# Feed-forward gradients turned by DMA instead of TensorE, and attention's output turned one stage earlier

## The chip, the cores and the metric

The kernel runs on one core of a Trainium2 chip. The metric is the device time of one execution in microseconds (us): before the change the median of three runs is 2908.62 us (2898.36 to 2910.74). PE is TensorE (PEld its weight loads), DVE is VectorE, ACT is ScalarE, POOL is GpSimd and SP is SyncE. SP and POOL also issue the transfers, each in its own order; a transfer that waits holds up all that stands behind it on the same queue. "Turned" means transposed: from token-major (a token per partition) to feature-major, or back.

## What is computed

The reference is one transformer layer and its gradient: 2048 tokens of width 448.

```python
def _fwd_reference(...):
    h = x + _A_ref(_layernorm(x), mem0, Wq, Wk, Wv, Wo)     # attention in 64 segments of 32 tokens; the first
                                                            # 8 output rows of a segment are the next one's memory
    g = silu(layernorm(h) @ w_gate)                         # 448 -> 1792
    u = layernorm(h) @ w_up
    return h + (g * u) @ w_down                             # 1792 -> 448

def reference(..., grad_out):
    out, vjp = jax.vjp(forward, x, mem0, Wq, Wk, Wv, Wo, w_gate, w_up, w_down)
    return out, *vjp(grad_out)
```

In the feed-forward block's backward pass the gradient dz = grad_out @ w_down.T gives the gradients of the gate's input (dgp) and of u (du); the gradient of the normed h is dgp @ w_gate.T + du @ w_up.T.

## The kernel before, in words

Everything is written out by hand in program order (`tc.manual_schedule()`), so the order in which the code issues work is the order of each engine's queue. There are four stages: the forward chain of attention, the feed-forward tiles (forward and backward in one), the backward chain of attention, and a tail of weight gradients.

*Forward chain* (`forward_chain`). 64 steps, one a segment, each depending on the step before through the memory rows; four steps make a token tile of 128. A step projects q, k and v (L561, L569), moves v's rows into the layout that attention reads (`v_shift`: some rows by copies on POOL, L527, some by small transfers on SP, L758; `v_b_rows`, L754, for the memory rows), computes scores and probabilities, multiplies with v (L932) and applies Wo (L690). At the end of nearly every step `w_turn` (L772) has SP turn two 128-column pieces of a weight matrix from DRAM by a transposing DMA; at the start of the next step `w_store` (L766) has POOL store the result, and waits for it. In a tile's first step POOL also loads the input rows `T.x2` (L814), in two buffers in turn; they are read in the third step of the next tile (`out_ev`). After a tile's fourth step POOL stores the tile's attention output feature-major (OTA, 1024 KB, L981).

*Feed-forward tiles* (`ffn_phase`). 16 tiles of 128 tokens, taken in the order ORD. The loop runs over i = 0 to 13; in pass i the tile t has its backward part, the next tile n1 its forward part, and tile n2 is loaded. On PE a pass is: `dz(t)` (16 matmuls, L1128), `down_mm(t)` (14, L1180, reads the turned z in `ff.zT`), `dh_out(t-1)` (L1225), `gate(n1)` and `up(n1)` (32, L1128), `dh_turn(t)` (28 transposes by PE of dgp and du, L1166, evicted by ACT to `ff.dgpT` and `ff.duT`, L1079), `dout_turn(n1)` and `hn_turn(n2)` (L1108), and `dh_mm(t)` (28 matmuls, L1208, 14 over dgpT and 14 over duT). DVE makes dgp (L1193) and du (L1196) in `grads(t)` after dz, and z (L1151) in `up(n1)`; it reads dh_mm's result in `dh_ln` (from L216 on). On SP a pass has the three loads of tile n2 (L1092 to L1095), then for i = 1 to 12 the transposing DMA of z into `ff.zT` (L1303), then for i = 3 to 13 `o_turn(3)`: up to three transposing DMAs (L1243), each of half a tile of OTA, 128 x 1024, from DRAM into one of three buffers, and on POOL a store of each into OTok, the token-major copy that the tail reads (L1244). POOL's other stores of a pass are DH and DHb (L1215, L1218), DGP and DU (L1194, L1197), HN, Zt and the output. In pass i = 2 `load_back` has SP turn Wo from DRAM for the backward chain (four transposing DMAs, L1053 and L1054), with a memset on POOL that waits for them (L1055). In pass i = 10 the backward chain's first loads are issued.

The two matmul sums of `down_mm` and `dh_mm` stand in two fixed PSUM banks (`k.fix`); `dgp`, `du`, `ff.dgpT`, `ff.duT` and `ff.zT` are one buffer each.

Of the kernel before, what the change touches and what calls it, by code (L numbers as in the profile page):

```python
# [10 lines left out]
BF16 = mybir.dt.bfloat16  # L11
# [4 lines left out]
P = 128  # L16
# [81 lines left out]
@43264 oA#1:8192 oB#1:2048  # L98
@54016 V_sb:4096 hA:2048
@61184 part:2048 partB:2048 Vev:2048 aT#1:1024  # L100
xtmp:1024x2 x2load:1024x2 P_sb1:1024 S_sb:640x2 maskr:640 maskf:160 hB#1:256
@76032 wturn:1792"""
FFN = """WdT:14336
h_ld:896x3 hn:1024x3 dout_ld#2:1024x2 dh_t:1792 lnb_prod:1792 lnb_t1:1792 dh_b:896 o_t:896x2
# [392 lines left out]
def forward_chain(k: _K, hA, NWIN, Wq_sb, Wk_sb, Wv_sb, Wo_sb, maskr, work, stage, ff, feed, srcs):  # L497
    nc, tc = k.nc, k.tc
# [132 lines left out]
    def b_units(t, which):  # L631
        W_sb = {"k": Wk_sb, "q": Wq_sb, "v": Wv_sb}[which]
        T = tiles[t]
        st = {}

        def stat(kc):
            return T.hB[0:DB, kc, :, :]

        def mm(ps, half, kcs=range(4)):
            if which == "v":  # L640
                proj_v(ps, stat, half, kcs)
            else:
                proj(ps, W_sb, stat, half, kcs)

        def u1():
            st["p0"] = ps1(FP32)
            mm(st["p0"], 0)

        def e1():
            tg = "bevv" if which == "v" else "bev"  # L650
            st["ev"] = stage.tile([P, GF], BF16, name=tg, tag=tg, bufs=2)
            A(st["ev"][:, 0:HB], st["p0"][:, :])

        def u2():
            st["p1"] = ps1(FP32)
            mm(st["p1"], 1, range(0, 2))

        def u3():
            mm(st["p1"], 1, range(2, 4))

        def e3():
            V(st["ev"][:, HB:GF], st["p1"][:, :])
            if which == "v":
                T.vB = st["ev"]
            else:
                nc.gpsimd.dma_start(out=dr["KtokB" if which == "k" else "QtokB"][t], in_=st["ev"][:])

        def ut():
            if which == "v":
                return  # L670
            pt = ps1(BF16)
            for j in range(NJ):
                nc.tensor.transpose(pt[:, j * P:(j + 1) * P], st["ev"][:, j * P:(j + 1) * P], ident[:, :])  # L673
            st["pt"] = [pt[:, half * HB:(half + 1) * HB].rearrange("p (j g t) -> p j g t", j=4, g=G) for half in range(2)]

        def et():
            if which == "v":
                return
            dst = stage.tile([P, MC, SEG], BF16, name=which + "B", tag=which + "B", bufs=2)
            for half in range(2):  # L680
                A(fm_view(dst, half, 0, SEG), st["pt"][half])
            setattr(T, which + "B", dst)
        return dict(u1=u1, e1=e1, u2=u2, u3=u3, e3=e3, ut=ut, et=et)
# [43 lines left out]
    def none_units():  # L727
        def f():
            pass
        return dict(u1=f, e1=f, u2=f, u3=f, e3=f, ut=f, et=f)  # L730
# [33 lines left out]
    def w_store():  # L764
        for w, c, b in held:
            nc.gpsimd.dma_start(out=dr["WT"][w][:, c:c + 2, :], in_=b)  # L766
        held.clear()

    def w_turn():
        w, c = ahead.pop(0)  # L770
        b = work.tile([P, 2, D], BF16, name="wturn", bufs=1)
        nc.sync.dma_start_transpose(out=b, in_=wsrc[w][:, c * P:(c + 2) * P])  # L772
        held.append((w, c, b))
# [29 lines left out]
    for s in range(NSEG):  # L803
# [3 lines left out]
        if r == 0:  # L807
            if t + 1 < NT:
                tiles[t + 1] = tok_tile(t + 1)
            T.aT = stage.tile([P, KC, P], BF16, name="aT_tile", tag="aT", bufs=2)  # L810
            T.oA = stage.tile([P, MC, P], BF16, name="oA", tag="oA", bufs=2)
            T.oB = stage.tile([P, MC, SEG], BF16, name="oB", tag="oB", bufs=2)
            T.x2 = work.tile([P, DP], BF16, name="x_t2", tag="x2load", bufs=2)
            nc.gpsimd.dma_start(out=T.x2[:, 0:D], in_=X2[t * P:(t + 1) * P, :])  # L814
            cur = o_units(t - 1) if t > 0 else none_units()
        else:
            cur = b_units(t + 1, "?kqv"[r]) if t + 1 < NT else none_units()

        def stat(kc):
            return hA[0:DB, kc, sl, :]  # L820
# [93 lines left out]
            (nc.gpsimd if final else nc.sync).dma_start(out=dr["Vtok"][s, gg], in_=V_sb[QB * gg:QB * gg + 48, :])  # L914
        if s != NSEG - 3 and ahead:
            w_turn()
        if s == NSEG - 3:
            next(feed)

# [63 lines left out]
        late2 = late  # L983
        late = cur

    assert not ahead and not held
    uo["e3"]()
    next(feed)
    uo["ut"]()
# [70 lines left out]
def ffn_phase(k: _K, WT, ff, work, mv2, rstd2, srcs, back):  # L1060
# [127 lines left out]
    def grads(t):  # L1188
        o = T[t]
        dg = work.tile([P, F], BF16, name="scr", bufs=1)  # L1190
        nc.vector.tensor_tensor(out=dg[:], in0=o.dz[:], in1=o.u[:], op=ALU.mult)
        o.dgp = work.tile([P, F], BF16, name="dgp", bufs=1)
        nc.vector.tensor_tensor(out=o.dgp[:], in0=dg[:], in1=o.sg[:], op=ALU.mult)  # L1193
        nc.gpsimd.dma_start(out=dr["DGP"][rows(t), :], in_=o.dgp[:])  # L1194
        o.du = work.tile([P, F], BF16, name="du", bufs=1)
        nc.vector.tensor_tensor(out=o.du[:], in0=o.dz[:], in1=o.g[:], op=ALU.mult)  # L1196
        nc.gpsimd.dma_start(out=dr["DU"][rows(t), :], in_=o.du[:])  # L1197

    def dh_turn(t):
        turn_f(T[t].dgp, ff.dgpT, (A, A))  # L1200
        turn_f(T[t].du, ff.duT, (A, A))
# [31 lines left out]
        A(dT[:], pt[:, 0:KC * P])  # L1233
        nc.gpsimd.dma_start(out=dr["doutT"][t], in_=dT[:])

    quarters = [(t, q) for t in range(NT) for q in range(2)]

    def o_turn(n):
        for t, q in quarters[:n]:
            b = ff.ot[len(quarters) % 3]  # L1240
            del quarters[0]
            cols = slice(q * 1024, (q + 1) * 1024)
            nc.sync.dma_start_transpose(out=b.rearrange("n (c p) -> n c p", p=P), in_=dr["OTA"][t][:, cols])  # L1243
            nc.gpsimd.dma_start(out=dr["OTok"][t][:, cols], in_=b)  # L1244
# [34 lines left out]
    for i in range(NT - 2):  # L1279
        t, n1, n2 = ORD[i:i + 3]  # L1280
        if i > 0:
            load(n2)
        if i == 2:
            load_back(k, WT["o"], srcs["o"], True)
        if i == NT - 6:
            next(back)
        if not 1 < i < NT - 2:
            turn_f(T[t].z, ff.zT, (A, A))
        dz(t)
        if i > 0:  # L1290
            dh_ln(t - 1)
        down_mm(t)
        if i == 0:
            rstd(NT - 1, NT)
        grads(t)
        if i > 0:
            dh_out(t - 1)
        gate(n1)
        down_ev(t)
        norm(n2)  # L1300
        up(n1)
        if 0 < i < NT - 3:
            nc.sync.dma_start_transpose(out=ff.zT, in_=T[n1].z)  # L1303
        if 2 < i < NT - 2:
            o_turn(3)
        if i == NT - 3:
            dout_turn(n1)
            hn_turn(n2)
            gate(n2)
            load_back(k, WT["v"], dr["WT"]["v"], False, 0, HC)  # L1310
            up(n2)
            load_back(k, WT["v"], dr["WT"]["v"], False, HC, 2 * HC)
            dh_turn(t)
            slope(n1)
            slope(n2)
        else:
            dh_turn(t)
            dout_turn(n1)
            hn_turn(n2)
            slope(n1)  # L1320
        dh_mm(t)
# [783 lines left out]
```

## Time and profile before

| | |
|---|---|
| Median of three runs | 2908.62 us (2898.36 to 2910.74) |
| The profiled execution | 2923.15 us, of it a span of 2921.0 us |
| Mean granted TensorE clock | 0.986 |
| PE / DVE / ACT / POOL busy | 93% / 53% / 37% / 28% of the span |
| Forward chain | about 73 to 963 us |
| Feed-forward tiles | about 963 to 1295 us |
| Backward chain, then tail | from about 1312 us, the tail from about 2236 us |

In the profile's rows "L1208" is line 1208 of the kernel before. A row of the timeline gives start, length, engine, line, operation, "written <- read" by the program's names, the count, and in brackets how long the engine sat idle before and what ended it. Names such as `arena` and `wall` are large areas in which tiles are placed by hand, so a row is told by its line. "SPq" rows are SP issuing a transfer; the transfer itself ends later. DMA share is the mean busy share of the 16 DMA engines, by the durations of their packets; it can go over 1.

### The profile page before, as it was taken

How to read it: one execution, taken by the hardware profiler on the slowest of the kernel's cores; microseconds unless marked ns; L12 is line 12 of the kernel's file. 1: busy time of each engine (PE TensorE's matmuls, PEld its weight loads, DVE VectorE, ACT ScalarE, POOL GpSimd, SP SyncE). 2: the span in 40 equal slices, each digit the busy share in tenths (PEclk: the TensorE clock that was granted, in tenths of full speed). 3: DMA queues.
4: the chain of work that ended last, by engine and by line, in shares of the span. 5: the costliest groups of instructions: out<-in, count | busy, mean ns of one | idle time of the engine just before them, and what ended most of it. 6: DMA issues, size and time to landing. Idle time of an engine off the chain costs nothing.

```text
span 2921.0 us, 104667 instructions
## 1 busy us (share of the span) xinstructions
PE 2724.9 (93%) x44420; PEld 1513.2 (52%) x44420; DVE 1560.8 (53%) x4196; ACT 1083.1 (37%) x2882; POOL 812.9 (28%) x1493
## 2 busy tenths in 40 slices
PE   3999999999999899998999999999998999989999
PEld 1555555555555445545555555555554554445444
DVE  4666666666666678866666665666664112111221
ACT  2444444444444545553443444344432111111110
POOL 2232223222222223322222222222222223323222
PEclk8999999999999999999999999999999999999999
DMA  9655556655556799995566556555667999999995
GB/s 270 152 157 167 150 160 158 167 150 151 167 148 164 250 227 232 244 280 146 156 171 170 150 162 179 152 152 160 174 156 250 315 208 223 189 193 229 214 201 106
DMA packets 674674, 544.23 MB, mean 186 GB/s; under 512 B 511520, under 2 KB 577808, under 8 KB 664672
## 3 DMA queue, kind: packets, MB, share of 16 engines
q1 hardware_dynamic: 617968, 322.70, 51.7%
q0 software_dynamic: 56240, 214.84, 22.5%
q8 instruction: 350, 5.73, 0.8%
q14 instruction: 116, 0.95, 0.1%
HBM read 160.11 MB, written 244.55 MB: 139 GB/s over the span
## 4 chain that ended last, share of the span: by engine, by line
PE 38%; DVE 9%; DMA 4%; issue 3%; ACT 1%; POOL 1%; SPq 1%; ACTq 0%; DVEq 0%; POOLq 0%
PE psf L1942 13%; PE psf L1415 8%; DVE arena L1378 5%; PE psf L1903 3%; PE psf L1724 3%; PE psf L1387 3%; PE psf L1955 2%; PE psf L1422 2%; ACT arena L1381 1%; DVE arena L1710 1%; DVE arena L1707 1%; DVE arena L1704 1%; PE psh L1750 1%; DVE rsum L1706 1%; PE psh L1880 1%
## 5 line engine op out<-in xcount | busy, mean ns | idle before, releaser
L1942 PE MATMUL psf<-wall,arena 128*128 128x512 bf16 (+1 forms) x1824 | 395.5, 375 | 14.0 <-DMA wall<-dKA 14.0
L524 ACT CAST arena<-psf 128x512 bf16<-128x512 f32 (+2 forms) x560 | 235.8, 453 | 361.6 <-PE psf L561 251.4
L1381 ACT CAST arena<-psf 128x256 bf16<-128x256 f32 (+1 forms) x597 | 233.4, 418 | 303.0 <-PE psf L1387 213.4
L1415 PE MATMUL psf<-wall,arena 128*32 128x448 bf16 x6144 | 333.6, 359 | 5.1 <-issue 4.2
L561 PE MATMUL psf<-wall,arena 112*32 112x512 bf16 x5120 | 309.1, 384 | 30.4 <-DMA wall<-in_A_Wk_dram 13.6
L1942 PEld LDWEIGHTS <-arena 128*128 128x128 bf16 x1824 | 176.6, 98 | 214.8 <-issue 22.7
L1830 DVE CAST arena<-psf 128x448 bf16<-128x448 f32 (+1 forms) x83 | 54.6, 658 | 436.4 <-PE psf L1942 284.0
L521 DVE CAST arena<-psf 128x512 bf16<-128x512 f32 (+2 forms) x432 | 191.7, 469 | 121.1 <-PE psf L561 83.9
L1415 PEld LDWEIGHTS <-arena 128*32 128x32 bf16 x6144 | 154.1, 97 | 121.5 <-issue 15.2
L561 PEld LDWEIGHTS <-arena 112*32 112x32 bf16 x5120 | 126.1, 97 | 161.7 <-issue 27.8
L1378 DVE CAST arena<-psf 128x256 bf16<-128x256 f32 (+1 forms) x339 | 164.6, 485 | 83.4 <-PE psf L1724 41.9
L1828 ACT CAST arena<-psf 128x512 bf16<-128x512 f32 (+1 forms) x75 | 42.1, 562 | 445.4 <-PE psf L1942 292.3
L569 PE MATMUL psf<-wall,arena 112*32 112x512 bf16 x2560 | 169.2, 385 | 10.8 <-DMA wall<-in_A_Wv_dram 10.8
L1775 POOL COPY arena<-arena 128x32 bf16<-128x32 bf16 x63 | 13.2, 210 | 529.0 <-DVE arena L1427 529.0
L1387 PE MATMUL psf<-wall,arena 128*32 128x512 bf16 x2560 | 156.6, 381 | 1.2 <-DVE arena L1427 1.2
L524 ACT COPY arena<-psh 40x160 bf16<-40x160 bf16 (+2 forms) x320 | 118.9, 399 | 97.6 <-PE psh L673 52.7
L690 PE MATMUL psf<-wall,arena 128*32 128x224 bf16 x5120 | 150.6, 269 | 0.6 <-issue 0.6
L1724 PE MATMUL psf<-arena 40*128 40x40 bf16 x6144 | 146.9, 178 | 3.1 <-DVE arena L1378 1.2
L1724 PEld LDWEIGHTS <-arena 40*128 40x128 bf16 x6144 | 125.7, 93 | 33.7 <-issue 15.0
L1378 DVE COPY arena<-arena 32x512 bf16<-32x512 bf16 x384 | 133.9, 349 | 8.8
L521 DVE COPY arena<-psh 128x512 bf16<-128x512 bf16 (+2 forms) x336 | 109.5, 342 | 37.0 <-PE psh L575 31.1
L1378 DVE COPY arena<-psf 128x192 f32<-128x192 f32 x64 | 22.9, 357 | 199.1 <-ACT arena L1381 199.1
(229 smaller groups left out, 4492.8 us busy)
## 6 DMA issues: line engine op xcount, KB each, us to landing
Vtok<-arena SPq DMA_DIRECT2D x126, 192.0 KB
KtokA<-arena SPq DMA_DIRECT2D x64, 256.0 KB
QtokA<-arena SPq DMA_DIRECT2D x64, 256.0 KB
OTA<-arena POOLq DMA_DIRECT2D x16, 1024.0 KB, 5.1
arena<-QtokA SPq DMA_DIRECT2D x128, 128.0 KB
arena<-KtokA SPq DMA_DIRECT2D x128, 128.0 KB
dVA<-arena POOLq DMA_DIRECT2D x16, 1024.0 KB, 5.1
dKA<-arena POOLq DMA_DIRECT2D x16, 1024.0 KB, 7.3
```

What stands on the lines that cost most here:

```text
L521: nc.vector.tensor_copy(out=out, in_=in_)
L524: nc.scalar.copy(out=out, in_=in_)
L561: nc.tensor.matmul(ps[32 * g:32 * g + 32, :], lhsT=stat(kc), rhs=W_sb[0:DB, kc, c0:c0 + HB], start=(kc == 0), stop=(kc == KC - 1))
L569: nc.tensor.matmul(ps[32 * g:32 * g + 32, :].rearrange("t (y d) -> t y d", y=2), lhsT=stat(kc), rhs=wv[:, x, :, half, e, :], start=(kc == ...
L690: nc.tensor.matmul(ps[32 * g:32 * g + 32, 0:2 * DB], lhsT=x, rhs=Wo_sb[:, c, a * 2 * DB:(a + 1) * 2 * DB], start=first, stop=last)
L1378: nc.vector.tensor_copy(out=out, in_=in_)
L1381: nc.scalar.copy(out=out, in_=in_)
L1387: nc.tensor.matmul(ps[32 * g:32 * g + 32, :], lhsT=stat(kc), rhs=WoT_sb[:, kc, c0:c0 + HB], start=(kc == 0), stop=(kc == KC - 1))
L1415: nc.tensor.matmul(pO[32 * g:32 * g + 32, 0:D], lhsT=ch(c), rhs=WT[:, c, :], start=(first and i < 4), stop=(last and i >= MC - 4), skip_gr ...
L1724: nc.tensor.matmul(po[:, n * L:(n + 1) * L], lhsT=lhs[b:b + L, lc:lc + P], rhs=rhs[b:b + L, hh, 0:L], start=True, stop=True)
L1903: nc.tensor.matmul(ps[:, 0:D], lhsT=stat[:, i, c * P:(c + 1) * P], rhs=Y[:, i, 0:D], start=(i == 0), stop=(i == kts - 1))
L1942: nc.tensor.matmul(ps[:, 0:N], lhsT=Hx[:, i, dc * P:(dc + 1) * P], rhs=X[:, i, b * N:(b + 1) * N], start=(i == 0), stop=(i == kts - 1))
```

## The change

1. In passes i = 1 to 12 (`byq`) `dh_turn(t)` is left out. SP turns dgp and du instead, by two transposing DMAs from SBUF to SBUF (128 x 1792 each), issued after the three loads and ahead of z's turn.
2. `o_turn(3)` in passes 3 to 13 becomes `o_turn(1)` in passes 3 to 6, for the last two tiles alone.
3. The other 14 tiles' O is turned in the forward chain: in each step of tiles 1 to 14 `o_piece` has SP turn a quarter of the previous tile's O (128 x 512) from SBUF, behind `w_turn`, into one buffer; `w_store` in the next step has POOL store it to OTok.
4. To make room for that buffer `T.x2` has one buffer in place of two, and its load moves from a tile's first step to its fourth.

```diff
-xtmp:1024x2 x2load:1024x2 P_sb1:1024 S_sb:640x2 maskr:640 maskf:160 hB#1:256
+xtmp:1024x2 x2load:1024 oturn:1024 P_sb1:1024 S_sb:640x2 maskr:640 maskf:160 hB#1:256
...
 (w_store)
         held.clear()
+        for t, c, b in heldo:
+            nc.gpsimd.dma_start(out=dr["OTok"][t][:, c * P:(c + 4) * P], in_=b)
+        heldo.clear()
+
+    heldo = []
+
+    def o_piece(t, c):
+        b = work.tile([P, 4 * P], BF16, name="oturn", bufs=1)
+        nc.sync.dma_start_transpose(out=b[:].rearrange("n (c p) -> n c p", p=P), in_=tiles[t].oA[:, c:c + 4, :].rearrange("p c n -> p (c n)"))
+        heldo.append((t, c, b[:]))
...
 (if r == 0)
-            T.x2 = work.tile([P, DP], BF16, name="x_t2", tag="x2load", bufs=2)
-            nc.gpsimd.dma_start(out=T.x2[:, 0:D], in_=X2[t * P:(t + 1) * P, :])
...
+        if r == 3:
+            T.x2 = work.tile([P, DP], BF16, name="x_t2", tag="x2load", bufs=1)
+            nc.gpsimd.dma_start(out=T.x2[:, 0:D], in_=X2[t * P:(t + 1) * P, :])
...
         if s != NSEG - 3 and ahead:
             w_turn()
+        if 0 < t < NT - 1:
+            o_piece(t - 1, 4 * r)
...
-    quarters = [(t, q) for t in range(NT) for q in range(2)]
+    quarters = [(t, q) for t in (NT - 2, NT - 1) for q in range(2)]
...
+        byq = 0 < i < NT - 3
...
         up(n1)
-        if 0 < i < NT - 3:
+        if byq:
+            nc.sync.dma_start_transpose(out=ff.dgpT, in_=T[t].dgp)
+            nc.sync.dma_start_transpose(out=ff.duT, in_=T[t].du)
             nc.sync.dma_start_transpose(out=ff.zT, in_=T[n1].z)
-        if 2 < i < NT - 2:
-            o_turn(3)
+        if 2 < i < 7:
+            o_turn(1)
...
-            dh_turn(t)
+            if not byq:
+                dh_turn(t)
```

More of the change, by code (lines that the diff above doesn't have):

```diff
@@ L100 @@
 @61184 part:2048 partB:2048 Vev:2048 aT#1:1024
[L101 removed]
+xtmp:1024x2 x2load:1024 oturn:1024 P_sb1:1024 S_sb:640x2 maskr:640 maskf:160 hB#1:256
 @76032 wturn:1792"""
@@ L984, in forward_chain @@
         late = cur
-    assert not ahead and not held
+    assert not ahead and not held and not heldo
     uo["e3"]()
```

## The prediction

> **What bounds the kernel now.** I read the page's engine and DMA rows first, then busy time by stretch, to see which engine fills each of the two stages that the change touches.
>
> ```profile
> span 2921.0 us, 104667 instructions
> PE 2724.9 (93%) x44420; PEld 1513.2 (52%) x44420; DVE 1560.8 (53%) x4196; ACT 1083.1 (37%) x2882; POOL 812.9 (28%) x1493
> DMA  9655556655556799995566556555667999999995
> ...
> 73.00:963.00 890.00, 849.36 (x17516) 492.06 (x17508) 571.42 (x1799) 423.24 (x1065) 262.42 (x527) 0.99 0.60 159
> 1101.08:1195.13 94.05, 94.05 (x654) 50.05 (x652) 77.35 (x132) 53.14 (x96) 29.41 (x55) 1.00 0.95 234
> ```
>
> The last two rows give a stretch's length, then PE, PEld, DVE, ACT and POOL busy time, clock, DMA share and GB/s. The first is the forward chain: PE busy 95% of it, DMA 0.60. The second is five whole feed-forward tiles, 18.81 us each: PE has no idle time at all, DVE has 15.5 us of work a tile, ACT 10.6, and the DMA engines are at 0.95. So PE is the bound in the tiles and DMA stands close behind it.
>
> Then one tile in order of time, from one dh_mm (L1208) to the next.
>
> ```profile
> 1174.26 1.73 PE L1166 MATMUL psh<-ident,arena 128*128 128x128 bf16 x28
> 1175.86 0.62 PE L1108 MATMUL psh<-ident,arena 128*128 128x128 bf16 x8
> 1176.32 5.46 PE L1208 MATMUL s_ps<-wall 128*128 128x448 bf16 x28
> 1176.40 2.15 SPq L1303 DMA_TRANSPOSE wall<-wall  x1
> 1178.65 5.84 SPq L1243 DMA_TRANSPOSE wall<-OTA  x3
> 1181.81 0.62 DVE L216 TENSOR_REDUCE lnb_m<-s_ps 128x1 f32<-128x448 f32 x1 [2.23 <-PE s_ps L1208]
> 1184.47 2.81 PE L1180 MATMUL s_ps<-wall 128*128 128x448 bf16 x14
> 1184.83 0.54 POOL L1244 DMA_DIRECT2D OTok<-wall  x1 [7.66 <-DMA wall<-OTA]
> 1186.67 1.09 DVE L1193 TENSOR_TENSOR arena<-arena 128x1792 bf16<-128x1792 bf16 x1
> 1187.35 5.88 PE L1128 MATMUL psf<-wall 128*128 128x448 bf16 x32
> 1187.68 1.08 DVE L1196 TENSOR_TENSOR arena<-arena 128x1792 bf16<-128x1792 bf16 x1
> 1188.61 0.54 POOL L1215 DMA_DIRECT2D DH<-arena  x1
> 1192.93 2.22 DVE L1151 TENSOR_TENSOR wall<-psf,arena 128x448 bf16<-128x448 f32 x4
> 1193.07 1.73 PE L1166 MATMUL psh<-ident,arena 128*128 128x128 bf16 x28
> ...
> 1195.13 5.46 PE L1208 MATMUL s_ps<-wall 128*128 128x448 bf16 x28
> ```
>
> I count time from E, the end of a dh_mm: 1176.32 + 5.46 = 1181.78. The gate gradient dgp (L1193) is ready at 1187.76 = E+5.98, the up gradient du (L1196) at E+6.98, z (the last L1151) at E+13.37. The 28 turns of dgp and du (L1166) start at E+11.29, and the next dh_mm starts at E+13.35.
>
> **What the tile loses.** L1166 starts at 1174.26 and the next PE work, L1108, at 1175.86: the 28 turns take 1.60 us of a full PE. Without them dh_mm could start at E+11.75 and a tile take 17.21 us. That is the most there is to gain, in 12 tiles 19.2 us. The four ACT evictions that go with them cost nothing now (ACT is 53.14 us busy of 94.05). DVE is next: its wait at L216, 2.23 us, shrinks by 1.60 to 0.63, so it still fits.
>
> **What the tile waits for instead.** dh_mm now reads dgpT and duT from two DMA turns on SP. It needs dgpT at E+11.75 and duT half a dh_mm (2.73) later, at E+14.48. The wait stands on PE with dh_mm behind it, and behind that dz and everything of the next tile. The nearest row is the turn of z: the same form, size and queue.
>
> ```profile
> 1176.50:1177.50 1.00, 1.00 (x7) 0.54 (x6) 0.96 (x2) 1.00 (x2) 0.54 (x1) 1.00 0.00 0
> 1177.50:1182.00 4.50, 4.50 (x26) 2.31 (x25) 2.23 (x3) 1.96 (x4) 0.00 (x0) 1.00 1.31 235
> 1182.00:1183.25 1.25, 1.25 (x9) 0.40 (x7) 1.25 (x6) 0.00 (x0) 0.00 (x0) 1.00 0.15 9
> 1183.25:1185.50 2.25, 2.25 (x14) 1.17 (x13) 2.14 (x4) 1.93 (x4) 0.54 (x1) 1.00 1.33 228
> 1047.00:1048.50 1.50, 0.71 (x5) 0.21 (x3) 0.42 (x1) 1.16 (x3) 1.50 (x1) 1.00 1.20 318
> ```
>
> z's turn is issued at 1176.40; the engines move nothing for 1 us, are full for 4.5 us (z's 448 KB, its store Zt of 448 KB and small stores), stop for 1.25 us, and only then go on with O's pieces, though these were issued long before. I read that as one turn after another with a pause between. So z lands 5.6 us after its issue. For dgp, with the DGP store beside it as Zt is beside z, 5.6 us gives E+11.6: just in time for E+11.75. For du I add the pause, 1.25, and 448 KB at some 268 GB/s (between the 228 and the 318 above), 1.7: 8.55 us after dgp, E+14.53 against the 14.48 needed. Then zT: ready at E+13.37, but it starts after duT and a pause, 1.4 us later than now, so it lands at E+20.4, where down_mm (L1180, at 1184.47 = E+2.69, so E+19.9 in a 17.21 us tile) wants it 0.5 earlier.
>
> The ends: nothing late, no wait. Or du as O's first piece goes now: it is 256 KB behind z, and POOL sees it at 1184.83, 8.43 us after z's issue; 0.7 us more for the larger du and 1.9 us (448 KB at 235 GB/s) for the DU store gives 11.0, so dh_mm ends at 5.98 + 11.0 + 2.73 = E+19.7, a tile 0.9 us slower than now. The stores will crowd more than now: POOL issues DH at 1188.61 only because O's stores wait ahead of it; with those gone DH and DHb leave up to 3 us earlier and DGP and DU at once, right on the two turns. On the other side SP loses O's three issues (5.84 us) and the tile 768 KB of loads and 768 KB of stores; the two turns bring 896 KB. I take 0.4 us of wait, near the sequence z-then-pieces without the extra store, since that is the same queue: 1.2 us gained in each of ten tiles, **-12.0 us**. Tile 10 also turns four pieces of V on SP just ahead of dgp; one more pause and piece, **+1.5 us**. The four O pieces left (tiles 3 to 6, one each) come after zT and delay no turn before E+6: nothing. At tile 13, where O's last pieces went, PE still turns: nothing.
>
> **The tile that loads Wo.** In tile 2 four turns of Wo stand on SP ahead of this tile's own.
>
> ```profile
> 1020.45 5.46 PE L1208 MATMUL s_ps<-wall 128*128 128x448 bf16 x28
> 1025.13 13.43 SPq L1053 DMA_TRANSPOSE wall<-in_A_Wo_dram  x3
> 1038.67 4.55 SPq L1054 DMA_TRANSPOSE wall<-in_A_Wo_dram  x1
> 1043.34 1.68 SPq L1303 DMA_TRANSPOSE wall<-wall  x1
> 1048.36 2.82 PE L1180 MATMUL s_ps<-wall 128*128 128x448 bf16 x14 [0.79 <-DMA wall<-wall]
> 1053.86 0.40 PE L1225 MATMUL psh<-ident,arena 128*128 128x128 bf16 x4 [2.67 <-DVE arena L1076]
> 1054.09 7.47 PE L1128 MATMUL psf<-wall 128*128 128x448 bf16 x32
> 1063.46 5.46 PE L1208 MATMUL s_ps<-wall 128*128 128x448 bf16 x28
> ```
>
> E here is 1025.91. Today only z's turn is held (it lands 5.0 us after issue: 1043.34 to the end of PE's wait at 1048.36), and tiles 2 and 3 together take from 1025.91 to 1068.92, 43.0 us; the 5.4 over two tiles of 18.81 come from the waits of 0.79 and 2.67 and from 32 matmuls in 7.47 us after them (5.88 in a steady tile), the clock having dropped. After the change dgp's turn stands behind Wo: SP starts Wo 1.6 us later against E (the tile before is shorter), E+0.8, is done 18.1 us later, and dgpT lands 5.0 us on, at E+23.9, against the E+11.75 wanted. duT follows by 2.7 at 26.6, dh_mm ends at 29.3, plus the 1.6 us of clock after such a pause: 30.9; tile 3 then takes 17.4 and has the waits of today no more, its stores being long out: 48.3. **+5.3 us** (3.0 without the lost clock and with du sooner; 7.8 if zT is late too).
>
> **The forward chain.** 56 steps each get one 128x512 turn on SP behind w_turn and one 128 KB store on POOL behind w_store. The trace has no turn of that size. Its issue lies between the 1.23 us minimum and the 1.99 us median of the 128x1024 pieces.
>
> ```profile
> L1243 SPq DMA_TRANSPOSE wall<-OTA x32: 1232/1992/3408, 1065.7 to 1246.3; - x32
> SPq L758 <- ACT arena L524: 167.4, 112, 6.0
> POOL arena L527 <- ACT arena L524: 156.5, 60, 4.8
> PE psf L932 <- DMA arena<-arena: 6.5, 11, 1.5
> 359.98 0.76 POOL L766 DMA_DIRECT2D WTd_v<-arena  x1 [3.21 <-DMA arena<-in_A_Wv_dram]
> 362.26 1.26 POOL L527 COPY arena<-arena 32x512 bf16<-32x512 bf16 x2 [1.52 <-ACT arena L524]
> ```
>
> Behind the turn on SP stand the moves of v rows (L754, L758); SP idles 2.6 us a step there (167.4 over 64 steps), which covers 1.4. Behind the store on POOL stands the copy of v (L527), with 2.6 us of idle a step; in the worst step shown w_store waits 3.21 us and only 1.52 are left, and O's store would take that. The cover ends at attention's matmuls (L932), which already wait for a v move in 11 steps, 0.59 us each. x2's load moves from a tile's first step to its last, behind one DVE wait, ahead of POOL's k and q copies; 0.54 us, hidden in the same idle time. Ends: nothing, a little below it since x2 leaves the step with the 1024 KB store of O; or 0.59 us in all 56 steps, 33 us. I take 0.2 us in the 14 steps that follow that store, **+3 us**, being nearest to the 11 of 61 that wait now.
>
> **Sum.** -12.0 + 1.5 + 5.3 + 3 = -2.2 us. The profiled execution took 2923.15 us, 14.5 above the runs' median of 2908.62; against itself it would give 2921, against the median 2906.4, which I predict. What a measurement of this kernel tells from no change is about 0.5%, 14.5 us (the runs shown spread over 12.4).
>
> **Rivals.**
> - *The turns are the new bound of the tile (slower).* Place: PE's wait ahead of dh_mm. It decides once duT lands over 10.1 us after dgp (18.81 - 5.98 - 2.73). For it: DMA share 0.95 and stores that now leave with the turns; against: z lands in 5.6 with a store beside it. At 11.0: 10 x 0.9 = 9, with 5.3, 2 for tile 10 and 3 in the chain +19: 2928 us. If the two turns simply took 5.6 each without overlap they would be there after 11.2. The Trainium skill, VectorE: DVE Perf Modes, "The three transpose paths", gives a 128x128 turn 390 ns on TensorE and 1309 ns by DMA and advises TensorE; by that 28 turns would be an estimated 36.7 us by DMA against 10.9 on PE, some 24 us more a tile. The trace has 28 on PE in 1.73 us and 14 by DMA landed in 5.0 to 5.6, so the advice leans the same way but not its figures.
> - *The chain pays (slower).* The added turn and store hold v's moves. At 0.4 us in 56 steps, +22, less the tiles' 5.2: +17, 2926 us. For it: the 0.59 us waits; against: 2.6 us of idle on both queues. The Trainium skill, DMA: Bandwidth & Descriptors, "Issuing engines are not separate DMA queues", has DMAs of all engines on the same 16; the share of 0.60 here leaves room.
> - *All hidden.* Ten tiles at 1.60, the Wo tile at its lower end, nothing else: -16 + 3 = -13, 2895.6 us. For it: the figures above miss by 0.05 and 0.5 us only; against: 0.95 of DMA.
>
> **How the numbers follow.** The sum as worked out 0.50 (own range 2897 to 2918); turns as the bound 0.18; chain 0.14; all hidden 0.14; else 0.04. Leaving a tenth out on each side gives 2890 to 2930. Over 0.5% slower is 2923: most of the two slow rivals and a tail of the first, 0.31. Over 0.5% faster is 2894: under half of the last rival and a little of the rest, 0.09. Within: 0.60.
>
> **What would show it.** Steps between L1208 starts in tiles 4 to 9 near 17.6 us, with PE waits on DMA of some 0.4 ahead of or inside dh_mm (over 1.6: first rival). Tile 2's dh_mm starting some 24 us after the one before ended, tile 3 without its waits. L932's waits on DMA near 9 us in all. The prediction is wrong if tiles stay at 18.8 or over, if tile 2 doesn't wait, or if the forward chain grows by over 10 us.

## The result, and the profile after

The changed kernel is slower: 2937.57 us median (2933.26 to 2949.09, eight runs) against 2907.74 us (2898.36 to 2925.11, eight runs) before, a ratio of 1.0108 with a 95% interval of 1.0086 to 1.0129, or +25 to +38 us. The forecast was 2906.4, with a range up to 2930.

The profiled execution took 2939.68 us, its span 2937.9. First the engine rows at the head of its page.

```profile
span 2937.9 us, 104129 instructions
PE 2721.9 (93%) x44084; PEld 1498.8 (51%) x44084; DVE 1562.9 (53%) x4196; ACT 1045.0 (36%) x2834; POOL 829.7 (28%) x1521
```

PE's busy time is 3 us below that of before, although 336 transposes of 57 ns, 19.2 us, are gone. So neither the removed work nor the whole time can be read from the share of 93%, which stands as it did. The stage has to be taken by itself. In both kernels I cut from the start of `down_mm` in pass 1 to its start in pass 13, twelve tiles; the columns are those of the prediction's first fence. Before:

```profile
1009.79:1240.98 231.19, 227.73 (x1561) 120.16 (x1560) 184.81 (x311) 127.55 (x228) 69.21 (x124) 0.99 0.94 230
```

After:

```profile
1012.45:1275.09 262.64, 222.79 (x1226) 104.14 (x1225) 184.89 (x311) 88.74 (x180) 57.02 (x101) 0.94 0.89 197
```

The twelve tiles take 31.45 us more, which is the whole of the difference between the medians (29.8). (The spans of the two profiled executions differ by 16.9 only: before's had 14.0 us of waits on dKA in its tail, in 7 places, that after's hasn't.) PE's idle time in them went from 3.46 to 39.85 us (+36.4). Its busy time fell by 4.9 only: 19.2 us of transposes are gone, and the work that is left takes 14.3 us more, at a granted clock of 0.94 instead of 0.99. So 31.45 is 36.4 of waits, less 19.2, and 14.3 of slower work. And the DMA engines moved less per second than before (197 against 230 GB/s), so it isn't a bandwidth that has been used up over the stage: it is one transfer that somebody waits for. The waits of PE name it.

```profile
PE s_ps L1221 <- DMA wall<-arena: 39.7, 15, 9.3
PE psf L945 <- DMA arena<-arena: 10.3, 20, 1.3
```

L1221 is `dh_mm` (L1208 before). It waits 39.7 us in 15 places for a turn that writes `ff.dgpT` or `ff.duT`; before it never waited for a transfer. L945 is attention's product with v (L932 before), 6.5 us in 11 places then. Now one tile in order of time, with the rows of PE, SP and POOL that matter (SPq rows are SP issuing; L1317 and L1318 turn dgp and du).

```profile
1101.55 2.81 PE L1193 MATMUL s_ps<-wall 128*128 128x448 bf16 x14
...
1104.42 5.88 PE L1141 MATMUL psf<-wall 128*128 128x448 bf16 x32
1104.90 2.31 SPq L1317 DMA_TRANSPOSE wall<-arena  x1
1105.13 0.54 POOL L1207 DMA_DIRECT2D DGP<-arena  x1 [0.87 <-DVE arena L1206]
1106.13 0.54 POOL L1210 DMA_DIRECT2D DU<-arena  x1 [0.46 <-DVE arena L1209]
...
1107.32 4.70 SPq L1318 DMA_TRANSPOSE wall<-arena  x1
...
1110.14 0.61 PE L1121 MATMUL psh<-ident,arena 128*128 128x128 bf16 x8
...
1112.89 5.70 PE L1221 MATMUL s_ps<-wall 128*128 128x448 bf16 x28 [2.14 <-DMA wall<-arena]
```

PE is done with everything ahead of `dh_mm` at 1110.75 and waits 2.14 us. The turn of dgp, issued at 1104.90, is there at 1112.89, 8.0 us later. The stores of DGP and DU leave 0.2 and 1.2 us behind it, each with as many bytes (448 KB) as the turn. The second turn occupies SP for 4.70 us where the first took 2.31. In ten of the twelve tiles the same span, from the turn's issue to the end of the wait, is 7.3 to 9.6 us, and there PE waits for duT in the middle of `dh_mm` only three times, 3.1 us in all. Steps between `down_mm` starts are 19.7 to 23.8 us against 18.81, without tiles 2 and 3.

The slower work stands right behind the waits. Pass 12 as a timeline row, and the stretch of that row (columns as above, the clock third from the end):

```profile
1265.23 7.16 PE L1221 MATMUL s_ps<-wall 128*128 128x448 bf16 x28 [2.94 <-DMA wall<-arena]
1265.23:1272.39 7.16, 7.16 (x29) 3.33 (x30) 1.75 (x2) 0.00 (x0) 0.00 (x0) 0.76 1.13 226
```

`dh_mm` took 5.46 us before. Of the ten steps without tiles 2 and 3, six have it work for 7.1 to 8.3 us, its waits not counted, and a clock of 0.86 to 0.92 over the whole tile; in the other four it works for 5.6 to 5.7 us and the tile's clock is 1.00. The 32 matmuls ahead of the wait take 5.88 us in every tile, as before.

Tile 2, where Wo's four turns (L1067 is the last) stand ahead on SP:

```profile
1043.40 4.27 SPq L1067 DMA_TRANSPOSE wall<-in_A_Wo_dram  x1
1047.78 1.55 SPq L1317 DMA_TRANSPOSE wall<-arena  x1
...
1049.78 3.50 POOL L1068 MEMSET wall<- 64x4096 bf16 x1 [25.85 <-DMA wall<-in_A_Wo_dram]
...
1051.94 6.80 PE L1221 MATMUL s_ps<-wall 128*128 128x448 bf16 x28 [9.30 <-DMA wall<-arena]
...
1054.30 0.54 POOL L1207 DMA_DIRECT2D DGP<-arena  x1
```

Here POOL is held by the memset (L1068), so DGP and then DU leave only from 1054.30 on, and the same turn of dgp takes 1051.94 - 1047.78 = 4.2 us. The tile of pass 11 is the other exception:

```profile
1234.69 2.23 SPq L1317 DMA_TRANSPOSE wall<-arena  x1
1234.92 0.54 POOL L1207 DMA_DIRECT2D DGP<-arena  x1 [1.48 <-DVE arena L1206]
1237.08 3.76 SPq L1318 DMA_TRANSPOSE wall<-arena  x1
1238.57 0.54 POOL L1210 DMA_DIRECT2D DU<-arena  x1 [3.11 <-DVE arena L1154]
...
1240.64 2.82 PE L1221 MATMUL s_ps<-wall 128*128 128x448 bf16 x14
...
1245.99 4.40 PE L1221 MATMUL s_ps<-wall 128*128 128x448 bf16 x14 [2.52 <-DMA wall<-arena]
```

The store of DU leaves 3.9 us behind the turn instead of 1.2; dgpT is there within 6.0 us (1240.64), and duT, which now has that store beside it, comes 11.3 us after the first issue. That contrast is what the theory rests on: 4.2 us with neither store beside the turn, at most 6.0 with one, 7.3 to 9.6 with two.

### The profile page after: what moved, and what is told of

The parts are those of the page before. It is cut to its first block, busy times and chain, and to the rows that moved or that the text cites. A ratio compares the mean times of both kernels' runs of the same rounds, so it can differ in the third digit from the quotient of the medians.

```text
span 2937.9 us, 104129 instructions
## 1 busy us (share of the span) xinstructions
PE 2721.9 (93%) x44084; PEld 1498.8 (51%) x44084; DVE 1562.9 (53%) x4196; ACT 1045.0 (36%) x2834; POOL 829.7 (28%) x1521
## 4 chain that ended last, share of the span: by engine, by line
PE 39%; DVE 9%; issue 3%; ACT 1%; DMA 1%; POOL 1%; SPq 0%; ACTq 0%; DVEq 0%; POOLq 0%
PE psf L1959 13%; PE psf L1432 8%; DVE arena L1395 5%; PE psf L1920 4%; PE psf L1741 3%; PE psf L1404 3%; PE psf L1972 2%; PE psf L1439 2%; ACT arena L1398 1%; PE psh L1767 1%; DVE arena L1727 1%; DVE arena L1721 1%; DVE arena L1724 1%; DVE rsum L1723 1%; PE psh L1897 1%
## 5 line engine op out<-in xcount | busy, mean ns | idle before, releaser
L561 PE MATMUL psf<-wall,arena 112*32 112x512 bf16 x5120 | 310.6, 384 | 27.6 <-DMA wall<-in_A_Wk_dram 12.2
L561 PEld LDWEIGHTS <-arena 112*32 112x32 bf16 x5120 | 126.8, 97 | 159.3 <-issue 25.9
L1221 PE MATMUL s_ps<-wall 128*128 128x448 bf16 x448 | 102.0, 390 | 40.5 <-DMA wall<-arena 39.7
```

The source lines that it names most:

```text
L561: nc.tensor.matmul(ps[32 * g:32 * g + 32, :], lhsT=stat(kc), rhs=W_sb[0:DB, kc, c0:c0 + HB], start=(kc == 0), stop=(kc == KC - 1))
```

## The experiments

The theory: in the tiles the landing of dgpT sets the time, and what makes it late is the stores of DGP and DU that run beside the turn. The rivals: the forward chain takes part of the loss; the turn by itself is too long; the clock that drops in PE's pauses is a cost of its own; the Wo tile carries it.

### Which half of the change costs

One half each: the chain's part alone (O turned in the forward chain, dgp and du still turned on PE), and the tiles' part alone (dgp and du by DMA, O's pieces left in the tiles as before).

```diff
 chain_only, against the changed kernel
-        if byq:
-            nc.sync.dma_start_transpose(out=ff.dgpT, in_=T[t].dgp)
-            nc.sync.dma_start_transpose(out=ff.duT, in_=T[t].du)
+        if 0 < i < NT - 3:
...
-            if not byq:
-                dh_turn(t)
+            dh_turn(t)
 tiles_only, against the kernel before
+        byq = 0 < i < NT - 3
+        if byq:
+            nc.sync.dma_start_transpose(out=ff.dgpT, in_=T[t].dgp)
+            nc.sync.dma_start_transpose(out=ff.duT, in_=T[t].du)
...
-            dh_turn(t)
+            if not byq:
+                dh_turn(t)
```

> O's pieces in the forward chain as changed, dgp and du still turned on PE. Theory (PE's waits for the two turns in the tiles cost the time, the chain little): 2 to 6 us over before, the tiles at 18.8 us as before since PE has no idle time there to give back. Rival (the chain pays): 15 us or more over before, the forward stage alone longer by that.

> The chain as before, so O's pieces stay in the tiles, three a tile; dgp and du turned by DMA. Theory (turns late): the pieces stand ahead of the turns on the same queue, so tiles of 21 to 24 us and 30 to 60 us over before. Rival (the chain pays): under 17 us over before.

The chain alone: 2907.78 us against 2906.86, ratio 1.0006 (0.9976 to 1.0037). The tiles alone, in two runs: 2962.69 against the same, ratio 1.0186 (1.0113 to 1.0259). The same twelve tiles, first of the chain's part alone:

```profile
1009.90:1239.92 230.02, 226.49 (x1561) 120.01 (x1560) 184.93 (x311) 127.55 (x228) 57.01 (x101) 1.00 0.67 177
```

and of the tiles' part alone, with its wait at `dh_mm` (L1208 in that kernel) in the fence behind it:

```profile
1008.37:1296.01 287.64, 220.93 (x1226) 103.12 (x1225) 184.71 (x311) 88.69 (x180) 70.84 (x127) 0.92 1.06 225
```

```profile
PE s_ps L1208 <- DMA wall<-arena: 66.6, 20, 11.2
```

All of the loss is in the tiles, and moving O's pieces out of them saves 25 of the 56.5 us that the DMA turns cost there (287.64 against 262.64). The chain's part costs nothing that can be measured; its interval leaves room for the 3 us of the forecast, not for 22. It also gains nothing by itself: with the DMA share in the tiles down from 0.94 to 0.67 a tile is still 18.81 us (1070.56 to 1089.37), because nobody on the path waited for those transfers. L945 waits 5.2 us in 12 places in the chain's part alone, and 10.3 in 20 in the changed kernel, whose chain is the same; so from one profiled execution to another that wait differs by 5 us with the same chain, more than it grew over before (from 6.5), and no cost of the added turn can be read from it.

### The stores beside the turn

Three kernels. In the first neither DGP nor DU is stored in tiles 1 to 12, in the second DU alone isn't; the rows in DRAM are filled behind the tiles from z's rows, so the gradients of w_gate and w_up (in the second of w_up alone) come from other data and only the tiles' stage is read. In the third both stores are issued behind z's.

```diff
 no_stores (no_du_store: the second store alone)
-        nc.gpsimd.dma_start(out=dr["DGP"][rows(t), :], in_=o.dgp[:])
+        if not 0 < t < NT - 3:
+            nc.gpsimd.dma_start(out=dr["DGP"][rows(t), :], in_=o.dgp[:])
...
-        nc.gpsimd.dma_start(out=dr["DU"][rows(t), :], in_=o.du[:])
+        if not 0 < t < NT - 3:
+            nc.gpsimd.dma_start(out=dr["DU"][rows(t), :], in_=o.du[:])
...
 late_stores, as no_stores, and behind up(n1) with its store of z
+            nc.gpsimd.dma_start(out=dr["DGP"][rows(t), :], in_=T[t].dgp[:])
+            nc.gpsimd.dma_start(out=dr["DU"][rows(t), :], in_=T[t].du[:])
```

> The changed kernel with the stores of dgp and du left out in tiles 1 to 12 (two of the weight gradients are then computed from other data, copied there after the tiles; that copy lengthens the run, so only the tiles' stage is read). Theory (the stores beside a turn hold back its landing): dgpT lands within 5.5 us of its issue, as in tile 2 of the changed kernel where no store ran beside it, PE's wait ahead of dh_mm falls under 0.5 us and steady tiles take 17.2 to 18.0 us. Rival (a turn of 448 KB takes 7 to 9 us by itself, whatever runs beside it): tiles stay at 19.7 to 23 us.

> After's kernel without DU's store in tiles 1 to 12, the store of DGP left where it is: the one store beside dgp's turn that the prediction had priced. The rows of DU in DRAM are filled after the tiles from z's rows, so w_up's gradient is computed from other data; only the tiles' stage is read. Without both stores no tile but tile 2 waited ahead of dh_mm; with both they waited 39.7 us in 15 places. Theory that the 448 KB transfers that run beside the turn share the engines with it, so each store adds about 448 KB at 230 to 320 GB/s, 1.4 to 1.9 us, to its landing: dgpT lands some 6 to 7.5 us after its issue, half of the waits are left (8 to 20 us beside tile 2's), steady tiles 17.5 to 19.5 us. Rival, that the prediction's figure was right for one store and only DU's store, or the pair, breaks it: no waits but tile 2's, tiles 17.2 us as without both stores. Second rival, that one store holds a turn as much as two: waits and tiles as in after (20 to 21 us).

> The changed kernel with the stores of dgp and du issued after the store of z, so after the two turns, beside z's turn. Theory (stores hold back a turn): the wait ahead of dh_mm falls under 1 us and one appears ahead of down_mm, where zT is wanted; 10 to 25 us over before. Rival (turns slow by themselves): the wait ahead of dh_mm stays at 2 us or more, 25 to 40 us over before.

Without both stores, the twelve tiles and one tile of them:

```profile
1006.86:1228.84 221.98, 209.44 (x1226) 101.08 (x1224) 184.81 (x311) 88.69 (x180) 44.36 (x77) 0.97 0.86 183
```

```profile
1072.19 2.81 PE L1193 MATMUL s_ps<-wall 128*128 128x448 bf16 x14
...
1075.55 1.52 SPq L1319 DMA_TRANSPOSE wall<-arena  x1
1077.17 3.42 SPq L1320 DMA_TRANSPOSE wall<-arena  x1
...
1081.23 5.46 PE L1223 MATMUL s_ps<-wall 128*128 128x448 bf16 x28
...
1089.39 2.81 PE L1193 MATMUL s_ps<-wall 128*128 128x448 bf16 x14
```

dgpT is there at most 5.7 us after the issue (1081.23 - 1075.55), `dh_mm` waits for nothing, runs through both halves without a break, and the tile takes 17.20 us (1089.39 - 1072.19), as most tiles of this kernel do. The only wait left ahead of `dh_mm` is tile 2's, 11.2 us. So the two turns by themselves are not too slow.

With the one store of DGP beside it (`dh_mm` is L1222, the turns L1318 to L1320):

```profile
1004.01:1250.36 246.35, 214.24 (x1226) 101.97 (x1225) 184.82 (x311) 88.72 (x180) 50.75 (x89) 0.97 0.89 188
```

```profile
1075.44 2.31 SPq L1318 DMA_TRANSPOSE wall<-arena  x1
1077.86 4.20 SPq L1319 DMA_TRANSPOSE wall<-arena  x1
1082.19 5.47 PE L1222 MATMUL s_ps<-wall 128*128 128x448 bf16 x28 [0.90 <-DMA wall<-arena]
...
1100.45 5.47 PE L1222 MATMUL s_ps<-wall 128*128 128x448 bf16 x28 [0.89 <-DMA wall<-arena]
```

The turn lands after 6.75 us (1082.19 - 1075.44), the wait is 0.9 to 1.1 us and the landing 6.75 to 6.9 in six tiles, and the tile 18.3 (1100.45 - 1082.19). In five others the wait is 1.5 to 4.3 us and the landing takes 7.4 to 10.3, as long as with both stores; in the two longest more stands close to the turn (in pass 10 V's four turns on SP right ahead, in pass 7 the stores OTok, DH and DHb within 0.7 us), and which of it delays the turn was not separated. So a single landing doesn't tell one store from two; the stage does. Without the stores, with DGP's, and with both it takes 221.98, 246.35 and 262.64 us, and PE's waits ahead of `dh_mm`, tile 2 left out, are 0, 20.1 and 30.4 us. Each of the two stores costs.

With both stores behind z's, the run is 2919.04 us against 2906.86 (ratio 1.0044, 1.0014 to 1.0074), 12 us over before where the changed kernel is 30, and the wait has moved:

```profile
1193.82 5.46 PE L1223 MATMUL s_ps<-wall 128*128 128x448 bf16 x28
1195.52 2.22 SPq L1323 DMA_TRANSPOSE wall<-wall  x1
...
1196.27 0.54 POOL L1319 DMA_DIRECT2D DGP<-arena  x1
...
1204.44 2.82 PE L1193 MATMUL s_ps<-wall 128*128 128x448 bf16 x14 [2.31 <-DMA wall<-wall]
```

`dh_mm` (L1223) no longer waits in a steady tile (0.7 us in one, beside tile 2's 12.0). Now z's turn (issued at 1195.52) has three 448 KB stores beside it, lands at 1204.44, 8.9 us later, and `down_mm` (L1193) waits for it, 18.6 us in ten places. In both places the stores hold back the turn that they run beside; no third place was tried.

### The clock, and the Wo tile

In `keep_warm` PE does 28 transposes that nobody reads, in place of the turns it was rid of, so that it doesn't stand still ahead of `dh_mm`. In `after_spread` Wo's four turns are issued one a pass in passes 2 to 5, behind z's turn and O's piece, and not all ahead of tile 2's turns.

```diff
 keep_warm
+            if byq:
+                for _ in range(2):
+                    pw = ps1(BF16)
+                    for j in range(7):
+                        for _ in range(2):
+                            nc.tensor.transpose(pw[:, j * P:(j + 1) * P], T[n1].hn[:, 0:P], ident[:, :])
+            else:
                 dh_turn(t)
 after_spread
-        if i == 2:
-            load_back(k, WT["o"], srcs["o"], True)
...
+        if 1 < i < 6:
+            wo_turn(i - 2)
```

> The changed kernel with 28 transposes of the normed rows on PE, written to a bank that nobody reads, where the 28 turns of dgp and du stood: PE is busy through most of its wait. Theory (PE's waits cost twice, once themselves and once by the clock that drops after them): the granted clock in the tiles goes back to 0.98 or more, dh_mm takes 5.5 us in every tile, and the time falls by 8 to 13 us against the changed kernel, to 18 to 23 us over before, though PE does 1.6 us more a tile. Rival (the waits alone, the clock drop is a part of no account): 28 to 45 us over before.

> The changed kernel with Wo's four turns one in each of tiles 2 to 5, behind the turn of z and O's piece, in place of all four in tile 2 ahead of dgp's. Theory (a turn waits for every turn ahead of it on SP): tile 2's dh_mm no longer waits some 9 us, tiles 2 and 3 take 40 to 43 us in place of 48.3, tiles 4 and 5 may gain a us of wait each: 20 to 27 us over before. Rival (Wo's turns cost their time wherever they stand): 29 to 33 us over before.

`keep_warm`: 2932.84 us against 2904.63, ratio 1.0098 (1.0063 to 1.0132). Its twelve tiles:

```profile
1013.68:1273.07 259.39, 233.45 (x1561) 119.92 (x1560) 184.87 (x311) 89.80 (x180) 57.19 (x101) 0.97 0.94 200
```

The clock rises from 0.94 to 0.97 and PE's idle time falls from 39.85 to 25.9 us, but its busy time grows by 10.7 (19.2 for the added transposes, 8.5 less for the rest), and the stage is only 3.3 us shorter (259.39 against 262.64). The 8 to 13 us expected of the whole run did not come. Tile by tile there is more to see. Tiles 2 and 10 are longer than in the changed kernel, where they took 27.99 and 20.47 us; here are both, and the rows of tile 10:

```profile
1033.85:1064.37 30.52, 21.77 (x131) 10.78 (x130) 15.44 (x27) 7.49 (x15) 7.72 (x9) 0.83 1.11 260
1204.69:1232.54 27.85, 20.88 (x131) 10.52 (x131) 15.46 (x27) 7.54 (x16) 4.30 (x8) 0.88 0.93 162
```

```profile
1208.86 4.13 SPq L1317 DMA_TRANSPOSE wall<-arena  x1
...
1222.43 7.42 PE L1221 MATMUL s_ps<-wall 128*128 128x448 bf16 x28 [6.97 <-DMA wall<-arena]
```

In tile 10 dgp's turn follows V's four turns on SP at once (1.2 us behind them in the changed kernel) and lands 13.6 us after its issue; whether the added transposes had a part in that isn't shown. The other ten tiles have a clock of 1.00 each and take 201.0 us against 214.2. So in the tiles the lowered clock is a loss of its own on top of the wait that brings it on: the slow matmuls are `dh_mm` and `dz`, behind the landing and ahead of the next dgp. That the whole run gains by a warm PE is not shown; its interval and that of the changed kernel overlap.

`after_spread`: 2932.99 us against 2904.63, ratio 1.0085 (1.0056 to 1.0113).

```profile
PE s_ps L1221 <- DMA wall<-arena: 25.7, 17, 3.9
```

Tile 2's wait of 9.3 us is gone and smaller ones stand in its neighbours. The intervals of this run and of the changed kernel overlap, so that anything is gained is not shown; the loss stays without the Wo tile's wait.

### Give the turn more time

If only the landing is at fault, a `dh_mm` that asks for dgpT later must lose its wait. In `half` du is turned by PE (14 transposes) and dgp by DMA, and `dh_mm` takes du first, so that dgpT is wanted 2.73 us later and no second turn follows. In `deferred` `dh_mm` is taken a pass later, behind the next dz, and `down_mm` behind the gate, with `dh_ln` and `dh_out` moved along; `deferred2` also turns dout ahead of `up`. `deferred_spread` and `deferred2_spread` add the spread of Wo's turns.

```diff
 half
-            nc.sync.dma_start_transpose(out=ff.duT, in_=T[t].du)
...
-            if not byq:
-                dh_turn(t)
+            if byq:
+                turn_f(T[t].du, ff.duT, (A, A))
+            else:
+                dh_turn(t)
...
-        dh_mm(t)
+        dh_mm(t, (1, 0) if byq else (0, 1))
 deferred (the order in a pass)
         dz(t)
-        if i > 0:
-            dh_ln(t - 1)
-        down_mm(t)
+        if i > 1:
+            dh_mm(t - 1)
...
         grads(t)
+        if i > 1:
+            dh_ln(t - 1)
...
         gate(n1)
+        down_mm(t)
...
-        dh_mm(t)
+        if not byq:
+            dh_mm(t)
 deferred2, beside it
+        dout_turn(n1)
         up(n1)
...
-            dout_turn(n1)
```

> After's kernel with dgp turned by DMA and du by PE (14 turns, 0.80 us), and dh_mm taking du first and dgp second. Own order of PE: a tile is 17.21 + 0.80 = 18.0 us, and dgpT is wanted 9.3 us after dgp is ready (12.55 + 2.73 - 5.98). Theory that the landing of dgpT beside the two gradient stores, 7.3 to 9.3 us in after, is what held the tiles: no or small waits (under 0.5 us a tile), tiles 18.0 to 18.4, tile 2 still waits for Wo's turns (6 to 9 us), the run 2903 to 2910 (ratio 0.998 to 1.001). Rival, that any DMA turn ahead of z's makes z late and down_mm waits in its place: waits of 1 us or more a tile at down_mm, tiles over 19, the run over 2918.

`half`: 2908.34 us against 2903.46, ratio 1.0023 (0.9999 to 1.0048).

```profile
1018.92:1250.45 231.53, 221.06 (x1394) 111.17 (x1393) 184.98 (x311) 108.10 (x204) 57.04 (x101) 0.99 0.83 200
```

```profile
1104.97 2.25 SPq L1318 DMA_TRANSPOSE wall<-arena  x1
1105.20 0.54 POOL L1207 DMA_DIRECT2D DGP<-arena  x1 [1.48 <-DVE arena L1206]
1106.20 0.54 POOL L1210 DMA_DIRECT2D DU<-arena  x1 [0.46 <-DVE arena L1209]
...
1112.06 5.47 PE L1222 MATMUL s_ps<-wall 128*128 128x448 bf16 x28 [0.41 <-ACT wall L1092]
```

With both stores at their old places no steady tile waits for the turn; only tile 2 does, 5.7 us. dgpT is wanted at 1112.06 + 2.73, 9.8 us after its issue, and is there. Every other wait ahead of `dh_mm` is 0.4 us for ACT's eviction of PE's last transposes; with it a tile is 18.61 us (1120.22 - 1101.62 between `down_mm` starts), and the twelve take 231.53, as long as before. The whole of the +31 us is gone. `half` alone doesn't say whether for the later moment or for the second turn that is left out; `deferred`, which keeps both turns, shows below that the later moment is enough. The upper end of the interval of `half` leaves open a loss of 0.5%, of which the tiles show nothing.

> The changed kernel with dh_mm of a tile put one pass later, behind the next tile's dz (down_mm behind the gate, dh_ln behind the next tile's dgp and du on DVE, dh_out ahead of up): dgpT is then wanted some 14 us after dgp, not 5.8. Theory (the turns are only late, not too many): steady tiles of 17.2 to 17.8 us without waits on a turn, a few us lost at tile 2: 5 to 14 us under before. Rival (the DMA engines or DVE are the bound of a tile with three turns): tiles stay at 18.8 us or over, and the time at or over before.

> The same with Wo's four turns one in each of tiles 2 to 5. Theory: 4 to 8 us under the former, so 9 to 20 us under before. Rival (DMA or DVE bound): no less than the former.

`deferred`: 2904.32 us against 2904.63, ratio 0.9999 (0.9979 to 1.0019). Of the waits for dgpT and duT one of 8.1 us in tile 2 is left and 0.5 beside it, yet a tile is 18.28 us and not 17.2, for a new wait:

```profile
PE psf L1141 <- ACT wall L1092: 13.0, 15, 1.4
```

dz follows at once on the transposes of dout that it reads, since `dh_mm` no longer stands between, and waits for their eviction by ACT, some 0.9 us a tile. `deferred_spread` has the same tile of 18.28 us and no wait in tile 2, and gains nothing: 2910.48 us, ratio 1.0028 (1.0001 to 1.0054).

> As in deferred (each tile's dh_mm taken one pass later, behind the next dz), but dout of the next tile is turned ahead of up and not right before dz, so that dz finds its input in place. In deferred a tile took 18.28 us and PE waited 13.0 us in 15 places for ACT's eviction of that turn. Theory that after the change a tile has 17.2 us of PE work and that only waits lengthen it: the waits of 13 us go, a tile takes 17.2 to 17.4, the run is 9 to 12 us shorter than deferred, about 2894 (ratio to before 0.995 to 0.997). Rival, that the DMA engines are the bound of a tile at about 18.3 us whatever the order on PE: tiles stay at 18.2 or more, with new waits on DMA ahead of dh_mm or down_mm, and the run stays at 2904 (ratio 1.000).

> deferred2 with Wo's four turns spread over passes 2 to 5, one each, behind z's turn. In deferred the one wait left at pass 2 was 8.08 us. Theory: that wait goes and each of the four tiles carries one more turn with room for it (dgpT now has a whole dz more, 2.9 us, to land): 3 to 8 us less than deferred2, ratio to before 0.992 to 0.996. Rival: four tiles at the brink each get a wait of 2 us or more, and nothing is gained against deferred2 (deferred_spread gained nothing against deferred).

`deferred2`: 2905.25 us against 2903.46, ratio 1.0006 (0.9988 to 1.0024). `deferred2_spread`: 2898.83 against the same, ratio 0.9994 (0.9979 to 1.0009). Five tiles of the latter:

```profile
1149.13:1235.88 86.75, 86.16 (x512) 41.91 (x511) 77.68 (x131) 36.93 (x75) 21.44 (x40) 1.00 0.96 220
```

That is 17.35 us a tile with PE busy 99% of it, and DVE 90%. The wait for ACT has shrunk to 1.8 us in three places and most tiles are at the 17.2 us that PE's work allows. But the room is used up: in three tiles (1083.11 to 1149.13, 22 us each) PE waits up to 2.4 us for DVE and 3.6 for a turn, and `deferred2` alone has 21.2 us of waits for turns in eight places, 9.3 of it in tile 2. So both readings expected were half right: 17.2 us tiles are there, and in between those that transfers stretch. No version here beats the kernel before by more than can be measured. In the profiled execution of `deferred2_spread` the twelve tiles are 7.9 us shorter than before (1012.59 to 1235.88), in the ratio of the runs there is no such gain; where the rest goes stays open.

## Why the prediction was wrong, by its own steps

*Where the time is lost: right as the first rival had it.* "The turns are the new bound of the tile (slower). Place: PE's wait ahead of dh_mm" is what happened, at a higher price than its 2928 us, and with dgpT late where that rival reckoned with duT. It had a chance of 0.18.

*What the tile loses: right.* Without its 28 transposes a tile takes 17.20 us where nothing is waited for (without the two stores), forecast 17.21.

*The step that failed* is "For dgp, with the DGP store beside it as Zt is beside z, 5.6 us gives E+11.6: just in time for E+11.75". With DGP's store alone of the two (`no_du_store`) the turn takes 6.75 to 6.9 us in six tiles and up to 10.3 in others; with what the kernel really issues there, the stores of both DGP and DU, 7.3 to 9.6. In the tile shown dgpT is there at E+14.0 (E = 1098.85) and PE was ready at E+11.9. The 5.6 us is the moment at which the DMA engines fall quiet behind z's issue; PE waited for nothing in that tile, so no row gives z's landing there. The one landing of z that PE did wait for, 5.0 us in tile 2, had no store of Zt beside it, which leaves 5.7 us after that landing:

```profile
1054.08 0.54 POOL L1152 DMA_DIRECT2D Zt<-wall  x1
```

The DU store was put on the account of duT alone (in the upper end of 11.0), though it leaves 1.2 us behind dgp's turn. The upper end was thus set on the wrong turn: of the 39.7 us of waits 34.1 are for dgpT, in eleven of twelve tiles, and 5.6 for duT, in four. For duT the 11.0 was a fair figure where the DU store ran beside it (11.3 in pass 11). "I take 0.4 us of wait ... 1.2 us gained in each of ten tiles, -12.0 us" became +26.1: those ten took 214.3 us against 188.2. That is 27.6 us in which PE stands still, less 16.0 of transposes, and 14.5 of slower work.

The Trainium skill bears on this in DMA: Bandwidth & Descriptors, "Issuing engines are not separate DMA queues": transfers of all issuing engines end up on the same 16 engines and interleave. The runs agree: stores issued by POOL delay a turn issued by SP, 4.2 us where they come later (tile 2), 7.3 to 9.6 beside them. The prediction used that section for the chain, where it cost nothing, and not for the tile. The Trainium skill, VectorE: DVE Perf Modes, "The three transpose paths", prices a DMA turn of 128x128 at 1309 ns, which would be an estimated 18.3 us for the 14 of one gradient. In the changed kernel the longest time from dgp's issue to the end of PE's wait is 9.6 us. (The prediction's "some 24 us more a tile" is 25.8 as the difference of its own two figures.) The advice of the Trainium skill to turn on TensorE (VectorE: DVE Perf Modes, "Rules for kernel authors") held here all the same: what decided was when the turn is wanted and what runs beside it.

*"The stores will crowd more than now": right, and weighed too low.* It was set against the 1536 KB a tile that the O pieces no longer move. That relief is real, 25 us between the tiles' part alone and the whole change, but against the wrong base: in the kernel before, O's pieces cost no tile anything (18.81 us with them, and in `chain_only` without).

*A slower PE: not foreseen outside tile 2, where it was put at 1.6 us.* The sum has no such term for the ten tiles, and there it is 14.5 us. It follows from the late landing: without the two stores the same ten tiles have a clock of 1.00. But it comes on top of the waits, as the ten tiles of `keep_warm` show.

*Tile 10, +1.5: not to be seen in the changed kernel.* That tile took 20.47 us, less than the mean of the ten, 21.4. In two other kernels it is seen, and is larger: with V's turns right ahead, dgp's turn lands after 10.2 us in `no_du_store` and 13.6 in `keep_warm`.

*The Wo tile, +5.3: right in sum, not in its parts.* Tiles 2 and 3 took 48.33 us from E to E (1030.75 to 1079.08), forecast 48.3. `dh_mm` of tile 2 ended 28.0 us after E and not 30.9, since dgpT came 4.2 us after its issue with no store beside it; tile 3 took 20.3 and not 17.4, since it had a wait of its own.

*The chain, +3: not to be told from nothing.* L945's waits are 10.3 us where about 9 were forecast, but 5.2 with the same chain in `chain_only`, whose time is that of before within 0.4%. The second rival, 22 us there, is excluded.

*Scatter and chances.* The base was right (2907.74, and 2908.62 when the sum was made). The range ended at 2930 since its slow rivals had duT at 11.0 and dgpT never late; the waits for dgpT in those ten tiles alone are 21.8 us.

## What to carry to other kernels

When work leaves an engine that is the bound and goes to a transfer, its price is the time from issue to landing in the traffic of that very moment, against the moment its reader wants it; take it from a row that has the same transfers beside it, and count every store that leaves within those microseconds, from any engine. A landing that is forecast to be just in time has no room for error: here 5.7 us fitted and 6.75 didn't. A wait can cost more than itself: here the matmuls behind many of them ran at a lower clock, 14.5 us in ten tiles beside 27.6 of waits. Before moving such work, give the reader more time: with `dh_mm` taking the DMA's half last, or a pass later, the same turns were hidden, and the tile then met the next limits (ACT's eviction, DVE) with little left to win.

## What the runs showed that was not expected

- A turn of 128x1792 lands 4.2 us after its issue with no large store beside it, 6.75 to 6.9 in six tiles with one of 448 KB (7.4 to 10.3 in five others), 7.3 to 9.6 with two. Whether the stores take a share of each engine or stand ahead of the turn in it was not separated.
- A second turn issued right behind the first holds SP for longer: in the tiles shown 3.42 us without stores, 4.20 with one and 4.70 with both, where the first takes 1.52 to 2.31. What SP waits for in it the profile doesn't show.
- A DMA share cut from 0.94 to 0.67 changed nothing in tiles that waited for no transfer (18.81 us both), while the 896 KB of stores that leave beside the turn cost 3.4 us a tile (262.64 against 221.98 in twelve) at a share of 0.89.
